# Moving the second keys' projection, four kinds of small work and seven last matmuls in an attention and FFT-filter kernel

## The chip, the cores and the metric

The kernel runs on one core of one Trainium2 chip. The time is the device time of one execution in microseconds (us): 424.93 is the median of three runs (424.67 to 424.96). Smaller is better. The core has five engines that run their own instruction lists in order and wait for each other by semaphores: PE (TensorE, matrix multiply), DVE (VectorE), ACT (ScalarE, here the exponentials), POOL (GpSimd) and SP (SyncE, here a queue that issues DMAs).

## The reference

`x` is 2048 tokens by 448 features, in bf16. Two branches are mixed by a gate:

```python
g = sigmoid((x * gate_w).sum(-1, keepdims=True))
# A: attention with 16 heads of 28
q, k, v = split(x @ wqkv)                 # (1, 16, 2048, 28) each
p = softmax(q @ k^T * 28 ** -0.5)
a = (p @ v, heads joined) @ wo
# B: a filter in the frequency domain
X = rfft2(x) * (w_r + 1j * w_i)           # (2048, 225)
b = irfft2(X).astype(bfloat16)
return g * a + (1 - g) * b
```

## The kernel before

**Attention.** The 16 heads are four groups `T` of four heads; a head is padded to 32 rows, so that a group fills 128 partitions. Queries are cut in four pieces of 512; a chunk `c` (0 to 15) is one group and one piece. For a chunk there are 16 blocks of 128 keys. A score tile is one key block, one head and 512 queries: one matmul that uses 32 rows of the PE array (`score`, L834), so that four of different heads run side by side. The scores of two or three tiles fill a PSUM buffer `ps2` or `ps3` (one of each), and one ACT instruction (L1092, in `exp`) exponentiates the whole buffer, 1024 or 1536 columns, into a tile in SBUF. There are 358 of these exponentials; "exp k" below is the k-th from 0, and "scores(k)" are the matmuls that fill its buffer. The even ones have 1536 columns and the odd ones 1024. Scores(k+2) need the buffer of exp k and so follow its end. Exponentiated tiles are multiplied with the values by four matmuls that use 32 columns each (`pv`, L1013, into the bank `psPV`). A part of the key blocks, "packs", is exponentiated on DVE instead: a score goes to a bank `bg`, L850 reads it, and a chain of DVE operations on 2048 columns follows (L870 to L904). For most packs its last addition is a DMA that POOL issues (L899).

**Other work** is cut in "units" with phases (`Unit`): a phase is a function `pe(ps)` that emits matmuls into a PSUM bank and a function `ve(ps)` that copies the result away, mostly on DVE. There are the banks `bg0` and `bg1`, and at the start also `pv`. `q`/`k` units project 512 tokens to queries or keys with four matmuls of 512 columns (`qk_unit`, L290) and one copy (L562); `first_unit` does so for group 0, with a square and a correcting matmul behind it (L614, L615, L619, L623). `T` units transpose x (L298, copied at L449). `V` units make the values of a block of 128 tokens with four matmuls of 336 columns (`v_unit`, L506) and one copy (L510). `f1`, `A`, `B`, `I` and `Z` units are the stages of the two FFTs; a `B` unit is L746 to L748 with two multiplications on DVE (L756, L758).

**The order** is decided when the program is built. `stream` goes through k: it emits exp k, some value matmuls (`do_pv`), then as many phases as a planner with assumed costs lets fit (`pick`, `step`), and then scores(k+2) (`scores`). `step` emits the matmuls and the copy at once, except for phases named in `BEHIND`: these are put in a list, `self.behind`, which is emitted behind the next scores. Matmuls on zeros fill holes that the planner sees and keep PE active: `until` and `dummy` call `one_zero` (L1328 and L1334), `zeros` adds one beside scores (L1049). None of them is read.

At the start of a group, `begin_group` spreads the projection's weights to the padded layout (`spread_w`, L285) with DVE copies; groups 1 to 3 have two such copies each. At a chunk's end `close_chunk` copies the sums out of `psPV` (L951), inverts the denominators (L961), multiplies them with the gate (L962, 128x16), and sends them by way of DRAM (SP, L966 and L975) to all rows; POOL then scales the chunk (L986, four instructions of 128x128).

Of the kernel before, what the change touches and what calls it, by code (L numbers as in the profile page):

```python
# [16 lines left out]
ALU = mybir.AluOpType  # L17
# [8 lines left out]
NT = 16  # L26
# [6 lines left out]
NC = 16  # L33
# [10 lines left out]
E_SC, E_EX, E_PV, E_PV2, E_MM = 0.32, 0.05, 0.33, 0.215, 0.22  # L44
# [8 lines left out]
BESIDE = 0.6  # L53
LATER = 70.0

BEHIND = {("T2.0", 1), ("T2.2", 1), ("q0.2", 1), ("f1.5", 1), ("I.0", 1), ("I.6", 1), ("base14", 3), ("out4", 3), ("out6", 2)}
NPT = 4
NPD = 5
CLAIM, LAST = 10, 8
# [105 lines left out]
class Kernel:  # L165
# [334 lines left out]
    def v_unit(self, t):  # L500

        nc = self.nc

        def pe(ps):
            for c in range(4):
                nc.tensor.matmul(ps[:, 0:D - DC], lhsT=self.xT[:, c, 128 * t:128 * t + 128],  # L506
                                 rhs=self.Wqkv[:, c, 2 * D + DC:3 * D], start=(c == 0), stop=(c == 3))

        def ve(ps):
            nc.vector.tensor_copy(out=self.vsb[:, t, 4:H, 0:DH],  # L510
                                  in_=ps[:, 0:D - DC].rearrange("p (h d) -> p h d", d=DH))
        return Unit(f"V{t}", [(pe, 0.68, 1344, ve, 0.42)], needs=["W3"])
# [41 lines left out]
    def qk_unit(self, T, q, b):  # L554
        nc = self.nc

        def pe(ps):
            self.project(ps, T, q, b)

        def ve(ps):  # L560
            dst = (self.kT if q else self.qT)[T][:, 512 * b:512 * b + 512]
            nc.vector.tensor_copy(out=dst, in_=ps[:])  # L562
            if b == 3:
                self.vq.insert(0, (squares, E_TT, None))

        def squares():
            sq = self.marks[f"sq{T}{q}"] = self.rot1.tile([P, S], BF16, name="sq")
            src = (self.kT if q else self.qT)[T][:]
            nc.vector.tensor_tensor(out=sq[:], in0=src, in1=src, op=ALU.mult)
            self.marks[f"sqt{T}{q}"] = self.tv + 0.1  # L570
        needs = [f"{'qk'[q]}{T}.{b - 1}"] if b else [f"Wg{T}"] if q else [f"kn{T}"]
        return Unit(f"{'qk'[q]}{T}.{b}", [(pe, 0.96, 2048, ve, 0.60)], needs=needs)

    def begin_group(self, T):

        self.new_group(T)
        for q in (1, 0):
            if T > 1:
                self.Wg[T, q] = self.Wg[T - 2, q]
            if T == 2 and q == 0:  # L580
                ones = self.Wg[T, q][:, 3, :].rearrange("p (s r) -> p s r", r=32)[:, :, KR:KR + 1]
                self.nc.gpsimd.memset(ones[96:P], 0.0)
            self.spread_w(T, q, self.nc.vector.tensor_copy)
            self.dve(0.20, True, self.tp)
        self.marks[f"Wg{T}"] = self.tv + 0.1
        if T == NG - 1:
            self.at(self.tv + 0.2, self.load_omg)
# [348 lines left out]
    def close_chunk(self, c):  # L936

        nc = self.nc
        T, qc = divmod(c, 4)
        if c == 12:  # L940
            assert all(n in self.marks for n in ("k3.3", "q3.3", "f1.15"))
            self.oT.append(self.per.tile([P, S], BF16, name="oT3", tag="xT_oT3"))
        if c >= TURN:
            f = self.rot2.tile([P, NT, 32], F32, name="ot", tag="o32")
            z = self.rot2.tile([P, NT, 32], BF16, name="oz", tag="sqh")
            self.dve(1.95)
            self.turned(c, f, z, 0, NT)
            self.marks[f"oT{c}"] = self.tv + 0.1
            return
        o32 = self.rot2.tile([P, QW], F32, name="o32")  # L950
        nc.vector.tensor_copy(out=o32[:], in_=self.psPV[:])  # L951
        r16 = self.rot2.tile([P, NT], F32, name="r16")
        nc.sync.dma_start(out=r16[:], in_=rows_of(o32[:, :], DH, 32, 4))
        st = {}

        def invert():
            if self.marks.get("gate", 1e9) > self.tv:
                self.at(self.tv + 3.0, invert)
                return
            i16 = self.rot2.tile([P, NT], F32, name="i16")  # L960
            nc.vector.reciprocal(out=i16[:], in_=r16[:])  # L961
            nc.vector.tensor_tensor(out=i16[:], in0=i16[:], in1=self.g16[:, qc, :], op=ALU.mult)  # L962
            self.dve(0.40)
            rD = self.dram.tile([4, QW], F32, name="rD")
            rv = rD[:]
            nc.sync.dma_start(out=_AP(tensor=rv.tensor, offset=rv.offset, ap=[[16, P], [1, 16]]), in_=i16[:])  # L966
            st["rv"] = rv
            self.at(self.tv + 3.0, spread)

        def spread():  # L970
            rep = st["rep"] = self.rot1.tile([P, QW], F32, name="rep", tag="rep")
            rv = st["rv"]

            for h in range(4):
                nc.sync.dma_start(out=rep[32 * h:32 * h + 32, :],  # L975
                                  in_=_AP(tensor=rv.tensor, offset=rv.offset + QW * h, ap=[[0, 32], [1, QW]]))

            self.at(self.tv + (8.0 if c < 12 else 5.0), lambda: self.jobs.append((self.tv + (8.0 if c < 12 else 2.0), scale)))

        def scale():  # L980
            o = self.oT[T][:, QW * qc:QW * qc + QW]

            nc.vector.memset(o[0:32, 0:4], 0.0)  # L983

            for e in range(0, QW, P):
                nc.gpsimd.tensor_tensor(out=o[:, e:e + P], in0=o32[:, e:e + P], in1=st["rep"][:, e:e + P], op=ALU.mult)  # L986
            self.tv += 0.07
            self.tg = max(self.tg, self.tv + 0.1, self.gen) + 1.27
            self.marks[f"oT{c}"] = self.tg + 0.1
        self.at(self.tv + 5.0, invert)  # L990
# [25 lines left out]
    def scores(self, k, end):  # L1016

        if self.act_c >= NC or not self.next_tile(k):
            return False
        t = self.tiles[k]  # L1020
        for c, i, _ in t:
            if c < 4:
                self.tp = max(self.tp, self.marks[f"q0.{c}"], self.marks[f"k0.{i // 4}"])
        start = max(self.tp, end + AP)
        if not self.away(start, [h for _, _, h in t]) and k > 1:
            self.zeros(start, [h for _, _, h in t])
        n = 2 if k % 2 else 3
        ps = self.psp.tile([P, n, QW], F32, name=f"ps{n}", tag=f"ps{n}", bufs=1)
        for _ in range(self.owed):
            self.nc.tensor.matmul(ps[:, 0, :], lhsT=self.warm[:], rhs=with_free(self.warm[:], [[0, 4], [1, P]]), start=True, stop=True)  # L1030
        self.owed = 0
        for e, (c, i, h) in enumerate(t):
            self.score(ps[:, e, :], c, i, h)
        self.ring[k] = ps
        start = max(self.tp, end + AP)
        self.tp = start + E_SC + (0.0 if isinstance(t[-1][1], int) else 0.1)
        self.add(self.tp, 128 * len(t))
        self.sc[k] = start + 0.50
        return True
# [200 lines left out]
    def step(self, u, b, limit):  # L1240
# [10 lines left out]
        ps = self.open[b][1]  # L1251
# [5 lines left out]
        if (u.name, len(u.phases)) in BEHIND:  # L1257

            self.behind.append(lambda: pe(ps))
            if ve is not None:  # L1260
                self.behind.append(lambda ve=ve: ve(ps))
                ve = self.later
            more = 1.0 if u.name == "T2.0" else 0.0
        else:
            pe(ps)
        self.tp = start + cost
# [2 lines left out]
        if ve is not None:  # L1269
# [7 lines left out]
            if u.name == "k0.1" and not u.phases and self.held:  # L1277
                self.held()
                self.held = None
                self.bank_free[0:2] = self.bank_free[1] + 0.6, self.bank_free[0]  # L1280
        if not u.phases:
            del self.open[b]
            if b == 2:
# [4 lines left out]

    def later(self, ps):
        pass  # L1290

    def take(self, u):

# [36 lines left out]
        self.dummies += 1  # L1330

    def one_zero(self):
        if self.pv_open and not self.ended:
            self.nc.tensor.matmul(self.psPV[:], lhsT=self.warm[:], rhs=with_free(self.warm[:], [[0, 4], [1, P]]), start=False, stop=False,  # L1334
                                  skip_group_check=True)
            self.add(self.tp + E_MM, 512)
# [31 lines left out]
    def stream(self):  # L1368
# [3 lines left out]
        self.fewer = self.begun = False  # L1372
        self.dummies = self.owed = 0
        self.ended, self.ot, self.held, self.next_exp = False, None, None, None
        self.behind = []
        self.pv_c, self.pv_free, self.pv_open = 0, 0.0, False
        for n in (3, 2):
            self.psp.tile([P, n, QW], F32, name=f"ps{n}", tag=f"ps{n}", bufs=1)
# [16 lines left out]
        k = -1  # L1395
        more = False
        while self.ring:
            k += 1
            if "T3.2" in self.marks and not more:
# [2 lines left out]
                e = self.per.tile([P, 14, QW], BF16, name="early2", tag="xtok_UT")  # L1402
                self.early[0].extend(e[:, 3 * j:3 * j + 3] for j in range(2))
                self.early[1].extend(e[:, 6 + 2 * j:8 + 2 * j] for j in range(4))
            self.exp(k)
            size = len(self.tiles[k])
            self.ta = end = max(self.ta, self.sc[k] + E_TAIL) + E_EXP[size]
# [22 lines left out]
            if self.act_c < NC:  # L1430
                self.until(end + AP)
            self.scores(k + 2, end)
            while self.behind:
                self.behind.pop(0)()
            self.fill_v(end - 0.2)
            self.log.append((k, end, self.tp, self.tv, len(self.vq), len(self.mand), self.dummies,
                             self.live, len([p for p in self.pieces if self.pack_t.get(p)]), self.pv_c))
# [222 lines left out]
```

## Time and profile before

| | |
|---|---|
| median of the runs | 424.93 us |
| the profiled execution's own time | 424.69 us |
| its span, first to last instruction | 422.9 us |
| busy: PE, ACT, DVE, POOL | 406.7, 411.5, 392.6, 61.3 us |
| exp 0 starts; exp 357 ends | 8.89; 416.56 us |
| ACT instructions of L1092 with tile `Pt` | 339, 385.6 us busy |
| TensorE clock granted | full in every slice |

The profile is of one execution, of which the span leaves out 1.8 us. The start of a row is when the engine began the instruction. ACT takes the next instruction in before the last one has ended, so that the durations of neighbours overlap; a matmul's duration (0.38 us at 512 columns) is modelled, and matmuls that follow each other without a wait start 0.215 us apart. "Idle before" counts only time in which no instruction of the engine was running.

### The profile page before, as it was taken

How to read it: one execution, taken by the hardware profiler on the slowest of the kernel's cores; microseconds unless marked ns; L12 is line 12 of the kernel's file. 1: busy time of each engine (PE TensorE's matmuls, PEld its weight loads, DVE VectorE, ACT ScalarE, POOL GpSimd, SP SyncE). 2: the span in 40 equal slices, each digit the busy share in tenths (PEclk: the TensorE clock that was granted, in tenths of full speed). 3: DMA queues.
4: the chain of work that ended last, by engine and by line, in shares of the span. 5: the costliest groups of instructions: out<-in, count | busy, mean ns of one | idle time of the engine just before them, and what ended most of it. 6: DMA issues, size and time to landing. Idle time of an engine off the chain costs nothing.

```text
span 422.9 us, 8345 instructions
## 1 busy us (share of the span) xinstructions
PE 406.7 (96%) x3196; PEld 144.5 (34%) x3196; DVE 392.6 (93%) x651; ACT 411.5 (97%) x369; POOL 61.3 (14%) x95
## 2 busy tenths in 40 slices
PE   8999999999999999999999999999999999999995
PEld 4343233333333333333333333333344332332232
DVE  6669989999899999999999999999999999999995
ACT  4999999999999999999999999999999999999994
POOL 6000002030100112012220100202002021310000
PEclk9999999999999999999999999999999999999999
DMA  9900301331302152375664446536553304233032
GB/s 234 180 8 2 8 27 31 90 72 32 76 15 47 24 101 59 73 169 103 153 154 96 105 103 117 112 71 109 111 146 81 77 2 91 49 76 78 22 74 67
DMA packets 32404, 34.30 MB, mean 81 GB/s; under 512 B 14988, under 2 KB 25228, under 8 KB 32332
## 3 DMA queue, kind: packets, MB, share of 16 engines
q1 hardware_dynamic: 28012, 20.21, 20.8%
q0 software_dynamic: 3600, 13.11, 17.1%
q8 instruction: 25, 0.41, 0.4%
q10 hardware_dynamic: 752, 0.44, 0.3%
q14 instruction: 15, 0.12, 0.1%
HBM read 14.85 MB, written 1.95 MB: 40 GB/s over the span
## 4 chain that ended last, share of the span: by engine, by line
PE 37%; ACT 30%; DVE 17%; issue 8%; DMA 6%; SPq 1%; DVEq 0%; ACTq 0%
ACT Pt L1092 28%; PE psPV L1013 7%; PE ps L834 6%; PE bg L834 4%; PE psPV L1334 4%; DVE Pd L850 4%; PE bg L290 3%; PE bg L1049 2%; DMA Fc<-cF 2%; DMA Wo<-in_A_wo_dram 2%; DVE pa L896 2%; ACT early L1092 2%; PE bg L678 1%; DVE U L689 1%; PE bg L506 1%
## 5 line engine op out<-in xcount | busy, mean ns | idle before, releaser
L1092 ACT ACTIVATE Pt<-ps 128x1024 bf16<-128x1024 f32 (+1 forms) x339 | 385.6, 1301 | 0.6 <-PE ps L834 0.2
L834 PE MATMUL ps<-qT,kT 32*128 32x512 bf16 (+2 forms) x926 | 143.3, 375 | 3.3 <-ACT Pt L1092 2.0
L850 DVE TENSOR_SCALAR Pd<-bg 128x512 uint16<-128x512 f32 x130 | 88.7, 683 | 5.0 <-PE ps L834 3.6
L1013 PE MATMUL psPV<-Pt,vsb 128*32 128x512 bf16 x818 | 79.9, 388 | 0.0
L834 PEld LDWEIGHTS <-kT 32*128 32x128 bf16 x1056 | 45.3, 91 | 93.7 <-issue 88.2
L899 POOL DMA_DIRECT2D Pd<-pa x25 | 23.7, 950 | 207.6 <-PE ps L834 89.0
L834 PE MATMUL bg<-qT,kT 32*128 32x512 bf16 x130 | 49.8, 383 | 1.2 <-DVE nM L651 0.4
L986 POOL TENSOR_TENSOR oT<-o,rep 128x128 bf16<-128x128 f32 x52 | 28.4, 572 | 132.3 <-DVE oT L983 73.2
L896 DVE TENSOR_TENSOR pa<-pa,n 128x2048 uint16<-128x2048 f16 (+2 forms) x33 | 40.1, 1214 | 0.6
L1013 PEld LDWEIGHTS <-vsb 128*32 128x32 bf16 x1008 | 23.1, 93 | 50.6 <-issue 50.0
L882 DVE TENSOR_TENSOR pa<-pa,n 128x2048 f16<-128x2048 f16 (+1 forms) x33 | 40.0, 1211 | 0.3
L1334 PE MATMUL psPV<-warm 128*128 128x512 bf16 x124 | 40.1, 385 | 0.0
L1049 PE MATMUL bg<-warm 32*128 32x512 bf16 x91 | 34.9, 383 | 1.4 <-DVE Pd L850 1.2
L290 PE MATMUL bg<-xT,Wg 128*128 128x512 bf16 (+1 forms) x112 | 29.6, 381 | 0.2
L873 DVE TENSOR_SCALAR Pd<-Pd 128x2048 uint16<-128x2048 uint16 (+1 forms) x33 | 23.2, 703 | 0.4
L870 DVE TENSOR_SCALAR n<-Pd 128x2048 uint16<-128x2048 uint16 (+1 forms) x33 | 22.5, 682 | 0.5
L689 DVE CAST U<-bg 128x450 bf16<-128x450 f32 x32 | 19.9, 622 | 3.1 <-PE bg L721 1.3
L885 DVE TENSOR_SCALAR pa<-pa 128x2048 f16<-128x2048 f16 (+1 forms) x33 | 22.5, 681 | 0.1
L878 DVE TENSOR_SCALAR pa<-n 128x2048 f16<-128x2048 uint16 (+1 forms) x33 | 22.3, 675 | 0.0
L1049 PEld LDWEIGHTS <-warm 32*128 32x128 bf16 x91 | 8.2, 90 | 29.0 <-issue 27.9
L787 PE MATMUL bg<-Binv,VT 128*128 128x448 bf16 x64 | 16.9, 355 | 0.2
L1092 ACT ACTIVATE early<-ps 128x1024 bf16<-128x1024 f32 (+1 forms) x13 | 15.3, 1264 | 1.0 <-PE ps L834 1.0
(189 smaller groups left out, 429.0 us busy)
## 6 DMA issues: line engine op xcount, KB each, us to landing
Pd<-pa POOLq DMA_DIRECT2D x25, 512.0 KB, 5.0
rep<-rD SPq DMA_DIRECT2D x52, 64.0 KB
CR<-cRB SPq DMA_DIRECT2D x8, 256.0 KB
UT<-U SPq DMA_DIRECT2D x16, 112.5 KB
VT<-U SPq DMA_DIRECT2D x16, 112.5 KB
CR<-cCS SPq DMA_DIRECT2D x8, 192.0 KB
xtok<-in_A_x_dram SPq DMA_DIRECT2D x3, 448.0 KB
out_dram<-fin SPq DMA_DIRECT2D x12, 112.0 KB
```

Source lines behind the costliest of these rows:

```text
L290: self.nc.tensor.matmul(ps[:], lhsT=self.Wg[T, q][0:k, c, :], rhs=self.xT[0:k, c, 512 * b:512 * b + 512], start=(c == 0), stop=(c == 3))
L689: self.nc.vector.tensor_copy(out=U[:], in_=ps[:, 0:F2])
L834: self.nc.tensor.matmul(out[:, w * j:w * j + w], lhsT=self.kT[T][32 * h:32 * h + 32, 128 * i:128 * i + 128], rhs=self.qT[T][32 * h:32 * h ...
L850: nc.vector.tensor_scalar(out=pk["t"][:, h, :], in0=ps[:], scalar1=SCALE * LOG2E * 512.0, scalar2=127.0 * 512.0, op0=ALU.mult, op1=ALU.add)
L882: v.tensor_tensor(out=st["a"], in0=st["a"], in1=st["n"], op=ALU.mult)
L896: v.tensor_tensor(out=q, in0=st["a"], in1=st["n"], op=ALU.mult)
L899: nc.gpsimd.dma_start(out=t, in_=q, accum_op=ALU.add)
L986: nc.gpsimd.tensor_tensor(out=o[:, e:e + P], in0=o32[:, e:e + P], in1=st["rep"][:, e:e + P], op=ALU.mult)
L1013: self.nc.tensor.matmul(self.psPV[32 * h:32 * h + 32, :], lhsT=self.vsb[:, i, 4 * T + h, :], rhs=pcs[h], start=first, stop=last, tile_posi ...
L1049: self.nc.tensor.matmul(ps[:], lhsT=self.warm[sl], rhs=with_free(self.warm[sl], [[0, 4], [1, P]]), start=True, stop=True, tile_position=(3 ...
L1092: self.nc.scalar.activation(out=Pt[:, 0:n, :], in_=ps[:, 0:n, :], func=ACT.Exp, scale=SCALE)
L1334: self.nc.tensor.matmul(self.psPV[:], lhsT=self.warm[:], rhs=with_free(self.warm[:], [[0, 4], [1, P]]), start=False, stop=False, skip_grou ...
```

## The change

It does four things.

1. `AFTER = {3: ("k0.1", 2)}`: scores(3) are held back until the second phase of the unit `k0.1` (the projection of tokens 512 to 1023 to keys) has been emitted; `T2.0` and, newly, `T3.0` are behind scores in that stretch. The zeros beside scores are left out up to k = 5.
2. `spread_w` of groups 1 to 3 (six copies) and the multiplication with the gate in `close_chunk` (13) go from DVE to POOL.
3. `SPARED`: one zero matmul less at each of the steps k = 0, 13, 116, 156 and 304. The planner counts it as if it were there. With the two that item 1 leaves out, the built program has seven matmuls fewer: three of L1328, two of L1334, two of L1049.
4. `ENDS`: of the units V5, V9, V15, q1.3, k2.1 and q3.0 the last of four matmuls, and of q3.2 the last two, are emitted behind the next scores, and with them the unit's copy on DVE.

The planner's decisions are otherwise the same: the same tiles stand in the same exp, and SP's list is the same. In the built order the exps concerned are those whose scores are emitted at that step: 2, 15, 118, 158, 306 (item 3) and 60, 75, 78, 88, 99, 208, 222 (item 4).

```diff
-BEHIND = {("T2.0", 1), ("T2.2", 1), ("q0.2", 1), ("f1.5", 1), ...
+BEHIND = {("T2.0", 1), ("T3.0", 1), ("T2.2", 1), ("q0.2", 1), ("f1.5", 1), ...
+SPARED = {0: 1, 13: 1, 116: 1, 156: 1, 304: 1}
+AFTER = {3: ("k0.1", 2)}
+ENDS = {"V5": 1, "V9": 1, "V15": 1, "q1.3": 1, "k2.1": 1, "q3.0": 1, "q3.2": 2}
...
-            self.spread_w(T, q, self.nc.vector.tensor_copy)
+            self.spread_w(T, q, self.nc.gpsimd.tensor_copy)
...
-            nc.vector.tensor_tensor(out=i16[:], in0=i16[:], in1=self.g16[:, qc, :], op=ALU.mult)
+            nc.gpsimd.tensor_tensor(out=i16[:], in0=i16[:], in1=self.g16[:, qc, :], op=ALU.mult)
...
-        if not self.away(start, [h for _, _, h in t]) and k > 1:
+        if not self.away(start, [h for _, _, h in t]) and k > max(AFTER) + 2:
             self.zeros(start, [h for _, _, h in t])
...
-        for e, (c, i, h) in enumerate(t):
-            self.score(ps[:, e, :], c, i, h)
+        def go():
+            for e, (c, i, h) in enumerate(t):
+                self.score(ps[:, e, :], c, i, h)
+        if k in AFTER:
+            self.after = k, go
+        else:
+            go()
...
+        elif u.name in ENDS:
+            n = 4 - ENDS[u.name]
+            pe(ps, range(n))
+            self.behind.append(lambda: pe(ps, range(n, 4)))
+            self.behind.append(lambda ve=ve: ve(ps))
+            ve = self.later
         else:
             pe(ps)
...
+        if self.after and AFTER[self.after[0]] == (u.name, len(u.phases) + 1):
+            k, go = self.after
+            self.after = None
+            go()
+            self.flush()
...
     def one_zero(self):
-        if self.pv_open and not self.ended:
+        if self.spare[self.k]:
+            self.spare[self.k] -= 1
+            self.add(self.tp + E_MM, 512)
+            self.dummies += 1
+        elif self.pv_open and not self.ended:
...
-            while self.behind:
-                self.behind.pop(0)()
+            if not self.after and k + 2 > min(AFTER) - 1:
+                self.flush()
```

More of the change, by code (lines that the diff above doesn't have):

```diff
@@ L54 @@
 LATER = 70.0
-BEHIND = {("T2.0", 1), ("T2.2", 1), ("q0.2", 1), ("f1.5", 1), ("I.0", 1), ("I.6", 1), ("base14", 3), ("out4", 3), ("out6", 2)}
+BEHIND = {("T2.0", 1), ("T3.0", 1), ("T2.2", 1), ("q0.2", 1), ("f1.5", 1), ("I.0", 1), ("I.6", 1), ("base14", 3), ("out4", 3), ("out6", 2)}
+SPARED = {0: 1, 13: 1, 116: 1, 156: 1, 304: 1}
+AFTER = {3: ("k0.1", 2)}
+ENDS = {"V5": 1, "V9": 1, "V15": 1, "q1.3": 1, "k2.1": 1, "q3.0": 1, "q3.2": 2}
 NPT = 4
@@ L502, in v_unit, with pe @@
         nc = self.nc
-        def pe(ps):
-            for c in range(4):
+        def pe(ps, part=range(4)):
+            for c in part:
                 nc.tensor.matmul(ps[:, 0:D - DC], lhsT=self.xT[:, c, 128 * t:128 * t + 128],
@@ L555, in qk_unit, with pe @@
         nc = self.nc
-        def pe(ps):
-            self.project(ps, T, q, b)
+        def pe(ps, part=range(4)):
+            self.project(ps, T, q, b, True, part)
         def ve(ps):
@@ L1290, in later, with flush @@
         pass
+    def flush(self):
+        while self.behind:
+            self.behind.pop(0)()
     def take(self, u):
@@ L1374, in stream @@
         self.ended, self.ot, self.held, self.next_exp = False, None, None, None
-        self.behind = []
+        self.behind, self.after = [], None
+        self.spare = dict.fromkeys(range(-1, 4 * NC * NT), 0) | SPARED
         self.pv_c, self.pv_free, self.pv_open = 0, 0.0, False
@@ L1404, in stream @@
                 self.early[1].extend(e[:, 6 + 2 * j:8 + 2 * j] for j in range(4))
+            self.k = k
             self.exp(k)
```

## The prediction

> **What bounds the kernel now.** I read the busy times first, then the groups of the exponentials, then the list of ACT's instructions one by one, and the timeline around each edit.
>
> ```profile
> PE 406.7 (96%) x3196; PEld 144.5 (34%) x3196; DVE 392.6 (93%) x651; ACT 411.5 (97%) x369; POOL 61.3 (14%) x95
> ...
> L1092 ACT ACTIVATE Pt<-ps 128x1536 bf16<-128x1536 f32 x170 | 257.4, 1514 | 0.5 <-PE ps L834 0.2
> ```
>
> ACT is busy 411.5 of 422.9 us, and the group shows only 0.5 us idle ahead of 170 exps. But idle time doesn't tell what a late exp costs, as neighbours overlap. In the list, a 1536-column exp that had to wait lasts 1.451 us and one that didn't up to 1.68; the ends are 1.343 apart (1536 columns) or 0.916 (1024), whichever it was. So a late start is free until the exp is at its least duration, and I count the **excess of ends**: the step from end to end beyond 1.343 or 0.916. Over all 358 exps it is 3.62 us; that is all that ACT's waits cost. At the exps that the change aims at it is, in us: exp 5 0.40, 15 0.14, 60 0.03, 75 0.04, 78 0.16, 79 0.08, 88 0.13, 99 0.10, 118 0.17, 158 0.02, 160 0.11, 208 0.23, 222 0.33, 306 0.00. PE and DVE are as full as ACT, so what is moved off one exp lands on the next.
>
> **Item 1, scores(3) behind the projection.**
>
> ```profile
> 13.20 0.69 DVE L614 CAST qraw<-bg 128x512 bf16<-128x512 f32 x1 [0.75 <-PE bg L290]
> 14.33 0.68 DVE L449 COPY xT<-pv 112x1024 bf16<-112x1024 bf16 x1
> 14.94 0.68 DVE L623 CAST kT<-bg 128x512 bf16<-128x512 f32 x1
> 15.21 1.02 ACT L1092 ACTIVATE early<-ps 128x1024 bf16<-128x1024 f32 x1 [0.29 <-PE ps L834]
> ```
>
> Exp 5 comes late because its scores, at 14.78, stand behind L619. The last L290 of k0.1 starts at 12.62, split off by scores(3). Unsplit, four matmuls run behind scores(2) (10.74): the last at 11.70, so L614 at 12.28, 0.92 earlier, and exp 5 is on time (-0.40). The transposes' copies (L449) then fill DVE from 13.41 to 14.70, so L623 starts at 14.70 instead of 14.94: only 0.24 of the 0.92 is left. Scores(6) need that kT: 15.67 becomes 15.43, and exp 6 follows by the head's 0.46 at 15.89. Exp 5's gain is kept only to that: **-0.24** (bounds 0 and -0.40).
>
> **Item 2, small pieces on GpSimd.** DVE loses 13 of L962 (0.175 each) and 6 of L285 (0.28 shown, steps of 0.18 to 0.28): about 2.8 to 4.0 us of 392.6. On POOL, idle 86%, a 112x448 copy took 0.56 in the head, and a 128x128 product (L986) 0.45 alone; a 128x16 product is not in the trace: between a small memset's 0.11 and 0.57. POOL runs in order, behind L899 (0.95) and L986; SP's send behind L962 gets its input 0.1 to 0.5 later, and L986, its reader, waits for DVE's L983 anyway (3.70 us at 89.16). The spread weights are needed 10 us or more after their copies. No exp's wait ends on these DVE pieces directly: **0** (bounds -0.3, and the rival's +0.4 below).
>
> **Item 3, five zeros.** k = 116:
>
> ```profile
> 142.81 0.81 PE L1328 MATMUL psPV<-warm 128*128 128x512 bf16 x3
> 143.55 0.39 PE L834 MATMUL ps<-qT,kT 32*128 32x512 bf16 x3
> ```
>
> Three zeros, 0.215 apart, delay scores(118); with two they start at 143.33, and exp 118's 0.17 goes: **-0.17**. k = 156: exp 158's 0.02 and part of exp 160's 0.11: **-0.07** (-0.02 to -0.13). k = 0: the zero in `pv` waits for a copy that ends at 10.37, and what remains starts no earlier: 0. k = 13: exp 15's 0.14 is an ACT instruction of its own (L491) between: 0. k = 304: scores(306) start 0.05 after exp 304's end, when their buffer comes free: 0.
>
> **Item 4, last matmuls behind scores.** Prices: full matmuls follow each other at 0.215 (512 columns) or 0.14 (336); changing between a full one and scores costs 0.31. So a split adds about 0.1 to PE, and takes 0.14 to 0.42 off the wait before the scores. The copy then comes after the scores and last matmul: 0.3 to 0.6 later. Whether that costs depends on who waits for the copy or for the bank.
>
> ```profile
> 245.91 0.38 PE L834 MATMUL bg<-qT,kT 32*128 32x512 bf16 x1
> 246.02 0.69 DVE L562 CAST qT<-bg 128x512 bf16<-128x512 f32 x1 [0.53 <-PE bg L290]
> 246.76 0.35 PE L746 MATMUL bg<-UT,CR 128*128 128x450 bf16 x1
> 247.24 0.39 PE L834 MATMUL ps<-qT,kT 32*128 32x512 bf16 x2
> ```
>
> - **q3.0.** Scores(208) go from 245.91 to 245.70: exp 208 gains its 0.23. But the last L290 goes from 245.60 to 246.02, behind them. L562 waits for it: 246.02 becomes 246.44, DVE already idle 0.53 there. Unit B's L746 uses the same bank and starts 0.05 after L562's end: 246.76 becomes 247.18. Scores(209) follow it: 247.24 to 247.66, scores(210): 248.21 to 248.63. Exp 210 now starts 0.52 after its scores' start, at 248.74 with 1.451, the least: it has no slack. It starts at 249.15: **+0.41**, exp 208's gain lost.
>
> ```profile
> 262.06 0.69 DVE L562 CAST qT<-bg 128x512 bf16<-128x512 f32 x1
> 262.82 0.36 PE L746 MATMUL bg<-UT,CR 128*128 128x450 bf16 x1
> 263.31 0.39 PE L834 MATMUL ps<-qT,kT 32*128 32x512 bf16 x2
> ...
> 264.21 0.39 PE L834 MATMUL ps<-qT,kT 32*128 32x512 bf16 x3
> ```
>
> - **q3.2**, two matmuls, again with a B unit on the same bank. L562 262.06 to 262.68, L746 263.44, scores(223) 263.93, scores(224) 264.83, exp 224 at 265.35 instead of 264.92, both by trace steps (rounded, +0.43 to 0.46): **+0.46**, exp 222's 0.33 lost.
>
> ```profile
> 77.42 0.50 DVE L510 CAST vsb<-bg 128x336 bf16<-128x336 f32 x1
> 80.30 0.68 DVE L562 CAST qT<-bg 128x512 bf16<-128x512 f32 x1
> 81.03 0.73 PE L506 MATMUL bg<-Wqkv,xT 128*128 128x336 bf16 x4
> 81.70 0.39 PE L834 MATMUL ps<-qT,kT 32*128 32x512 bf16 x3
> ```
>
> - **V5.** Exp 60 gains 0.03. L510 goes from 77.42 to 77.75; DVE has no gap up to L562 (80.30), which frees the bank for L506: 81.03 to 81.36, scores(64) 81.70 to 82.03, exp 64, with 0.03 of slack, +0.27: **+0.24** (0 if DVE's 0.33 is absorbed).
> - **V9**: its copy has DVE backlog ahead of it: 0. **V15**: 0.13 gained at exp 88, 0.07 of PE and a copy behind L882 to be made up by exp 90: 0 (-0.13 to +0.08).
> - **q1.3.** Exp 78 waits for value matmuls that free its `Pt` tile, not for scores; these (97.80) go behind the split, 98.0: **+0.20** (0 to +0.3).
> - **k2.1.** Exp 99's wait on PE is over at 122.20, yet it starts at 122.54. The same 0.34 stands ahead of exp 227 (268.21, 268.55), with 256 ACT instructions between and instruction fetches beside both. So earlier scores gain nothing, and the keys' copy, 122.01 to 122.30, reaches exp 103: **+0.15** (-0.10 to +0.25). [...]
>
> **Sum:** -0.24 -0.17 -0.07 +0.24 +0.20 +0.15 +0.41 +0.46 = **+0.98**. The profiled execution, 424.69, becomes 425.67; the median, 0.24 higher, 425.9.
>
> **Rivals.**
> 1. *All covered* (faster). The late copies and the bank cost nothing, because lighter DVE and earlier PE work run ahead to the next exps, and each exp aimed at gains its excess: 0.40 + 0.03 + 0.04 + 0.16 + 0.13 + 0.10 + 0.17 + 0.02 + 0.23 + 0.33 = 1.61; 423.3. It decides if exps 209, 210, 223 and 224 have 0.4 of slack. For: the start-by-start gaps really stand there. Against: exps 210 and 224 are at their least duration.
> 2. *Only the q3 units cost.* The 0.59 of V5, q1.3 and k2.1 is absorbed, since DVE has 3 us less to do: 425.3, no change or near its edge. For: V9 shows such slack. Against: DVE has no gap from 77.4 to 81.3.
> 3. *Port* (slower still). GpSimd's new pieces slow the DVE operations beside them:
>
> ```profile
> 89.16 2.15 POOL L986 TENSOR_TENSOR oT<-o,rep 128x128 bf16<-128x128 f32 x4 [3.70 <-DVE oT L983]
> 90.16 0.83 DVE L885 TENSOR_SCALAR pa<-pa 128x2048 f16<-128x2048 f16 x1
> 91.03 1.36 DVE L896 TENSOR_TENSOR pa<-pa,n 128x2048 uint16<-128x2048 f16 x1
> ```
>
> L885 takes 0.68 elsewhere and L896 1.22: 0.15 each, 0.19 on average over the 13 DVE operations that stretch. For 17 pieces that fall beside packs that is 3.2, 0.4 more than the 2.8 taken off: 426.3. It decides if each new piece meets a pack. [...]
> 4. *It doesn't do what it says:* exps 5 and 118 don't move. That is in the bounds of items 1 and 3.
>
> **How the numbers follow.** The sum as worked out 0.53; only q3 costs 0.20; the port 0.10; all covered 0.17. A measurement of this kernel can tell about 0.2%, 0.85 us, from no change: faster is under 424.08, slower over 425.78. The forecast lies close above the bound: of its 0.53, 0.42 slower and 0.11 same; of the second 0.16 same, 0.04 slower; the port slower; all covered 0.15 faster, 0.02 same. Together faster 0.15, same 0.29, slower 0.56. The range, 424.3 to 426.8, leaves out most of the fourth case and the worst ends of the bounds (k2.1 and q1.3 at their upper ends with the port).
>
> **What would show it.** Right: exp 5 without idle time; scores(118) at their buffer's release; L562 of q3.0 and q3.2 after 0.9 and 0.6 of idle DVE, L746 at about 0.05 after them, and exps 210 and 224 at 1.451 with an excess of ends of some 0.4; exps 64, 78 and 103 later; exp 99 still 0.34 after its wait; POOL with 19 instructions more; the total excess of ends 4.6 instead of 3.62. Wrong: L746 on time, or exps 209 to 210 and 223 to 224 with durations over the least. Then the sum falls by up to 0.87, to no change; and if exps 64, 78 and 103 stay on time too, it is faster.

## The result and the profile after

The changed kernel's median is 426.11 us over 18 runs; the kernel before had 424.88 in 18 runs beside it. The ratio of the runs is 1.0038, with a 95% interval from 1.0026 to 1.0049 (three of the 18 took 428 to 430 us; the medians alone give 1.0029). Forecast was 425.9, slower.

The profiled execution took 426.14 us, with a span of 424.1. Of its distance to the profiled execution of before, 0.16 us lies ahead of the first exp: its first exp ends at 10.51 instead of 10.35, as the transposes of x ahead of it (L347) took longer (the median of the first eight was 0.314 us instead of 0.219), and nothing of the change stands there (over the ten profiled executions that end lies between 10.35 and 11.42). Another 0.31 lies outside the span (2.09 us against 1.78), where no row shows what it is. So I compare from the end of the first exp to the end of the last, where nothing of this shows: the changed kernel needs 0.95 us more there. The sum had said 0.98.

The busy times on the page, and the two groups of exponentials with their shapes kept apart (busy us, mean ns of one, idle us before them and what ended it), after:

```profile
PE 407.0 (96%) x3189; PEld 145.3 (34%) x3189; DVE 390.5 (92%) x632; ACT 411.3 (97%) x369; POOL 71.4 (17%) x114
```

```profile
L1103 ACT ACTIVATE Pt<-ps 128x1536 bf16<-128x1536 f32 x170 | 259.9, 1529 | 0.6 <-PE psPV L1019 0.3 <-PE ps L840 0.2
L1103 ACT ACTIVATE Pt<-ps 128x1024 bf16<-128x1024 f32 x168 | 185.3, 1103 | 1.2 <-PE ps L840 1.0
```

The 1024-column group before:

```profile
L1092 ACT ACTIVATE Pt<-ps 128x1024 bf16<-128x1024 f32 x168 | 183.0, 1089 | 0.0
```

L1103 is the old L1092, L840 the old L834. POOL has its 19 instructions more, PE seven fewer. The idle time ahead of the 1536-column exps hardly changed (0.5 us before), but ahead of the 1024-column ones there is now 1.2 us idle instead of none, of which 1.0 ended with scores. The excess of ends over all exps is 4.57 us (3.62 before, 4.6 forecast). The timeline shows where the 1.0 is. Around q3.0:

```profile
245.97 0.38 PE L840 MATMUL bg<-qT,kT 32*128 32x512 bf16 x1
...
246.30 0.39 PE L296 MATMUL bg<-xT,Wg 128*128 128x512 bf16 x1
...
246.73 0.69 DVE L568 CAST qT<-bg 128x512 bf16<-128x512 f32 x1 [0.36 <-PE bg L296]
...
247.47 0.35 PE L752 MATMUL bg<-UT,CR 128*128 128x450 bf16 x1 [0.45 <-DVE qT L568]
...
247.95 0.39 PE L840 MATMUL ps<-qT,kT 32*128 32x512 bf16 x2
...
248.44 2.47 ACT L1103 ACTIVATE Pt<-ps 128x1024 bf16<-128x1024 f32 x2 [0.49 <-PE ps L840]
```

The last matmul stands behind the scores, the copy waits for it, the B unit's first matmul (L752) waits 0.45 us for the copy, scores(209) stand behind that, and ACT is idle 0.49. Up to here ACT is 0.28 later than before (end of exp 207); less that, the rows of L296, L568, L752 and scores(209) are at 246.02, 246.45, 247.19 and 247.67, where the prediction had 246.02, 246.44, 247.18 and 247.66. One sign of it is missing: DVE is idle 0.36 before L568, not 0.9, because the copy moved back in DVE's list too, and the operation of a pack that used to follow it (0.68 us) now runs first. Around q3.2 the chain is the same:

```profile
262.62 0.60 PE L296 MATMUL bg<-xT,Wg 128*128 128x512 bf16 x2
...
263.26 0.69 DVE L568 CAST qT<-bg 128x512 bf16<-128x512 f32 x1 [0.62 <-PE bg L296]
...
264.01 0.35 PE L752 MATMUL bg<-UT,CR 128*128 128x450 bf16 x1 [0.45 <-DVE qT L568]
...
264.98 2.37 ACT L1103 ACTIVATE Pt<-ps 128x1024 bf16<-128x1024 f32 x2 [0.51 <-PE ps L840]
```

### The profile page after: what moved, and what is told of

Same layout as the page of the kernel before. It is cut to its first block, busy times and chain, and to the rows that moved or that the text cites. A ratio compares the mean times of both kernels' runs of the same rounds, so it can differ in the third digit from the quotient of the medians.

```text
span 424.1 us, 8334 instructions
## 1 busy us (share of the span) xinstructions
PE 407.0 (96%) x3189; PEld 145.3 (34%) x3189; DVE 390.5 (92%) x632; ACT 411.3 (97%) x369; POOL 71.4 (17%) x114
## 4 chain that ended last, share of the span: by engine, by line
PE 46%; ACT 31%; DVE 13%; issue 7%; DMA 1%; SPq 1%; DVEq 0%; ACTq 0%
ACT Pt L1103 27%; PE psPV L1019 8%; PE ps L840 8%; PE bg L840 4%; PE psPV L1364 4%; PE bg L296 4%; PE bg L1060 3%; DVE Pd L856 3%; PE bg L512 2%; ACT early L1103 2%; PE bg L684 2%; DVE pa L902 1%; DVE U L695 1%; ACT oT L1103 1%; PE bg L718 1%
## 5 line engine op out<-in xcount | busy, mean ns | idle before, releaser
L1103 ACT ACTIVATE Pt<-ps 128x1024 bf16<-128x1024 f32 (+1 forms) x339 | 385.5, 1315 | 1.9 <-PE ps L840 1.2
L840 PE MATMUL ps<-qT,kT 32*128 32x512 bf16 (+2 forms) x926 | 142.8, 375 | 3.6 <-ACT Pt L1103 2.0
L1019 PE MATMUL psPV<-Pt,vsb 128*32 128x512 bf16 x818 | 79.9, 388 | 0.0
L840 PEld LDWEIGHTS <-kT 32*128 32x128 bf16 x1056 | 45.8, 91 | 95.2 <-issue 89.4
L840 PE MATMUL bg<-qT,kT 32*128 32x512 bf16 x130 | 49.8, 383 | 1.2 <-DVE nM L657 0.3
L1019 PEld LDWEIGHTS <-vsb 128*32 128x32 bf16 x1008 | 23.1, 93 | 50.4 <-issue 49.7
L888 DVE TENSOR_TENSOR pa<-pa,n 128x2048 f16<-128x2048 f16 (+1 forms) x33 | 39.9, 1208 | 0.3
L296 PE MATMUL bg<-xT,Wg 128*128 128x512 bf16 (+1 forms) x112 | 30.1, 381 | 0.6 <-DVE Pd L856 0.3
L879 DVE TENSOR_SCALAR Pd<-Pd 128x2048 uint16<-128x2048 uint16 (+1 forms) x33 | 23.7, 719 | 0.4
L891 DVE TENSOR_SCALAR pa<-pa 128x2048 f16<-128x2048 f16 (+1 forms) x33 | 22.4, 680 | 0.1
L884 DVE TENSOR_SCALAR pa<-n 128x2048 f16<-128x2048 uint16 (+1 forms) x33 | 22.4, 679 | 0.0
L968 POOL TENSOR_TENSOR i<-i,g 128x16 f32<-128x16 f32 x13 | 6.4, 491 | 88.5 <-DVE i L967 81.6
```

The lines of the kernel that those rows point to most:

```text
L296: self.nc.tensor.matmul(ps[:], lhsT=self.Wg[T, q][0:k, c, :], rhs=self.xT[0:k, c, 512 * b:512 * b + 512], start=(c == 0), stop=(c == 3))
L840: self.nc.tensor.matmul(out[:, w * j:w * j + w], lhsT=self.kT[T][32 * h:32 * h + 32, 128 * i:128 * i + 128], rhs=self.qT[T][32 * h:32 * h ...
L888: v.tensor_tensor(out=st["a"], in0=st["a"], in1=st["n"], op=ALU.mult)
L1019: self.nc.tensor.matmul(self.psPV[32 * h:32 * h + 32, :], lhsT=self.vsb[:, i, 4 * T + h, :], rhs=pcs[h], start=first, stop=last, tile_posi ...
L1103: self.nc.scalar.activation(out=Pt[:, 0:n, :], in_=ps[:, 0:n, :], func=ACT.Exp, scale=SCALE)
```

## Experiments

In each run I read the step of every exp's end against another kernel's, as in the prediction; each kernel has one profile, and nearly all steps that an edit leaves alone repeat within 0.02 us from kernel to kernel, while medians move by some tenths. Runs 1 to 4 were made together, and 5 to 8.

**1. Item 4 undone.**

```diff
-ENDS = {"V5": 1, "V9": 1, "V15": 1, "q1.3": 1, "k2.1": 1, "q3.0": 1, "q3.2": 2}
+ENDS = {}
```

> The changed kernel without item 4: all seven units emit their four matmuls and the copy at once. My theory (item 4 is what makes it slower; items 1 and 3 gain 0.24 + 0.24, item 2 nothing): 0.48 us below the kernel before, 424.4; exp 208 and exp 222 again late by 0.23 and 0.33 in their ends, exps 209 and 223 with no excess. Rival (the pieces on GpSimd slow DVE beside them): it stays above the kernel before, 425.2 to 425.6. Second rival (gains of items 1 and 3 are eaten before the end): 424.9.

Measured: 424.31 us, the kernel before 424.88; the ratio 0.9989 has an interval (0.9970 to 1.0007) that takes in no change, so the steps decide: from the first exp to the last it takes 0.84 us less than the kernel before. Exp 5 gains 0.40 and exp 6 gives 0.18 back; exps 118 and 160 gain 0.17 and 0.11; and two gains I had not counted, 0.07 at exp 126 and 0.17 at exp 222, come from item 2 (run 5). The excess at 209 and 223 is gone. Item 4 alone turns a gain into the loss.

**2. q3.0 and q3.2 whole, the other five split.**

```diff
-... "k2.1": 1, "q3.0": 1, "q3.2": 2}
+... "k2.1": 1}
```

> The changed kernel with q3.0 and q3.2 unsplit, the other five splits kept. My theory (each q3 split gives 0.23 or 0.33 at its exp and takes 0.6 at the next): 0.86 us less than the changed kernel, 425.2 to 425.3; excess of ends at exps 209, 223 and 227 about 0, 0 and 0.02. Rival (the five small splits cost most of it): not more than 0.3 below the changed kernel, 425.8.

Measured: 424.98 us, 1.13 below the changed kernel, and 1.02 in steps. Exp 209 is 0.60 earlier, 223 0.62, 227 0.19; exp 208 loses its 0.23, exp 222 only 0.16, since the other 0.17 had come with item 2. The rival of the small splits falls, though they too cost 0.67 (this run against run 1; 0.77 in steps).

**3. A decoy: the same PE list, but no copy waits behind scores.**

```diff
+        elif u.name in ("q3.0", "q3.2"):
+            n = 4 - ENDS[u.name]
+            pe(ps, (0, 1, 3) if n == 3 else (0, 3))
+            for _ in range(4 - n):
+                self.behind.append(self.zero_behind)
...
```

(`zero_behind`, left out here, is one matmul on zeros into `psPV`.)

> The changed kernel, with q3.0 and q3.2 doing one and two of their matmuls less (a part of the projection is left out), the copy emitted straight behind the ones that remain, and as many matmuls on zeros put behind the scores: PE's list has the same instructions in the same places, but the copy waits for no matmul behind the scores. My theory (the copy, and the bank it holds for unit B, is what costs): exps 208 and 222 keep their gain, exps 209 and 223 lose at most 0.1 instead of 0.6, B's first matmul stands within 0.1 of its place before; 1.0 us below the changed kernel, 425.1, 0.1 to 0.3 below the kernel that leaves the q3 units whole. Rival (it is PE's changes between score and full matmuls that cost): as slow as the changed kernel, 426.1, with exps 209 and 223 late by 0.5 or more.

Measured: 424.96 us, 1.15 below the changed kernel and level with run 2. Its timeline around q3.0:

```profile
245.97 0.39 PE L840 MATMUL ps<-qT,kT 32*128 32x512 bf16 x3
246.07 0.69 DVE L568 CAST qT<-bg 128x512 bf16<-128x512 f32 x1 [0.31 <-PE bg L296]
246.29 0.39 PE L1365 MATMUL psPV<-warm 128*128 128x512 bf16 x1
...
246.94 0.36 PE L752 MATMUL bg<-UT,CR 128*128 128x450 bf16 x1
```

The zero (L1365) stands where the projection's matmul stood, and PE changes between scores and full matmuls as often. But L568 starts 0.66 earlier and L752 0.53 earlier, without a wait, and exps 209 and 223 are 0.52 and 0.51 earlier than in the changed kernel. So of the 0.60 and 0.62 there, 0.5 is the copy and the bank. The rest is PE: against run 2, exp 209 keeps 0.08, 210 0.06, 223 0.11 and 227 0.19. I had expected the decoy to beat run 2 by 0.1 to 0.3, and it doesn't: PE's share alone eats the 0.22 and 0.16 that exps 208 and 222 gain.

**4. The q3 splits alone, on the kernel before.**

```diff
+ENDS = {"q3.0": 1, "q3.2": 2}
...
+        elif u.name in ENDS:
+            n = 4 - ENDS[u.name]
+            pe(ps, range(n))
+            self.behind.append(lambda: pe(ps, range(n, 4)))
+            self.behind.append(lambda ve=ve: ve(ps))
+            ve = self.later
```

> The kernel before with the splits of q3.0 and q3.2 alone. My theory: +0.86 us over the kernel before, 425.7, nearly all of the loss; exp 209 and 223 late by 0.6 in their ends. Rival (the loss comes from the sum of the small splits, or only together with the pieces on GpSimd): within 0.3 us of the kernel before.

Measured: 425.87 us, ratio 1.0026 (1.0015 to 1.0036). From first to last exp +0.87, with the steps of the changed kernel (-0.23, +0.61, +0.06; -0.33, +0.62, +0.20, -0.07). They need nothing of the rest of the change.

**5. Item 2 alone, on the kernel before.**

```diff
-            self.spread_w(T, q, self.nc.vector.tensor_copy)
+            self.spread_w(T, q, self.nc.gpsimd.tensor_copy)
-            nc.vector.tensor_tensor(out=i16[:], in0=i16[:], ...
+            nc.gpsimd.tensor_tensor(out=i16[:], in0=i16[:], ...
```

> The kernel before with item 2 alone (the 19 small pieces on GpSimd). My prediction's own value: no difference, 424.9. What the run without item 4 suggests: exps 126 and 222, which wait for work behind DVE's queue, gain 0.07 and 0.17, 0.25 us below the kernel before, 424.65. [...]

Measured: 424.80 us beside 425.00, not told apart by the medians. The steps: exps 126, 215 and 222 gain 0.07, 0.03 and 0.17, exp 178 loses 0.06, which the other kernels with these pieces do not show; from first to last exp 0.19 shorter. No step can be put down to pieces that hold up DVE. The long operations and the pieces, in this run:

```profile
L888 DVE TENSOR_TENSOR pa<-pa,n 128x2048 f16<-128x2048 f16 x32 | 38.9, 1214 | 0.3
...
L891 DVE TENSOR_SCALAR pa<-pa 128x2048 f16<-128x2048 f16 x32 | 22.0, 686 | 0.1
...
L968 POOL TENSOR_TENSOR i<-i,g 128x16 f32<-128x16 f32 x13 | 6.4, 491 | 89.5 <-DVE i L967 82.5 <-issue 6.8
...
L291 POOL COPY Wg<-Wqkv 112x448 bf16<-112x448 bf16 x6 | 3.8, 653 | 13.3 <-DMA Wqkv<-in_A_wqkv_dram 13.2
```

L888 and L891 took 1227 and 689 ns on average in the kernel before (as L882 and L885). But the means hide that the two engines do hold each other up:

```profile
75.20 0.62 DVE L649 TENSOR_REDUCE m<-bg 128x1 f32<-128x512 f32 x1
75.37 0.21 POOL L968 TENSOR_TENSOR i<-i,g 128x16 f32<-128x16 f32 x1 [2.27 <-DVE i L967]
...
107.09 0.85 POOL L291 COPY Wg<-Wqkv 112x448 bf16<-112x448 bf16 x1
107.33 1.17 DVE L879 TENSOR_SCALAR Pd<-Pd 128x2048 uint16<-128x2048 uint16 x1
...
227.09 1.16 DVE L888 TENSOR_TENSOR pa<-pa,n 128x2048 f16<-128x2048 f16 x1
227.25 1.07 POOL L968 TENSOR_TENSOR i<-i,g 128x16 f32<-128x16 f32 x1 [4.26 <-DVE i L967]
```

Beside a DVE operation that reads a PSUM bank, a product (L968) takes 0.21 or 0.22 us, little more than its 0.175 on DVE; that is so six times (twice the operation comes in only towards the end). The other seven times DVE was at work on 2048 columns in SBUF, and the product ended 0.07 after that operation, after up to 1.07 us. The other way round, L879 came while a copy (L291) was running and took 1.17 us instead of 0.68, and L884, at 108.84, took 0.88 instead of 0.68. These two cost DVE 0.7 us, against the 4.0 taken off it, and no exp is later for them.

**6. The five small splits as decoys.**

```diff
-... "k2.1": 1, "q3.0": 1, "q3.2": 2}
+... "k2.1": 1}
...
+            pe(ps, (0, 1, 3))
+            self.behind.append(lambda: self.zero_behind(336 if u.name[0] == "V" else 512))
-            pe(ps, range(n))
-            self.behind.append(lambda: pe(ps, range(n, 4)))
-            self.behind.append(lambda ve=ve: ve(ps))
-            ve = self.later
```

> The changed kernel without the q3 splits, and with V5, V9, V15, q1.3 and k2.1 doing three of their four matmuls (a quarter of each product is left out), the copy at once behind these, and one matmul on zeros of the same width behind the scores: PE's list as in the kernel with the five small splits. My theory: the copies' delay is what costs at V5 and k2.1, so that exps 64 and 103 lose at most 0.1 each instead of 0.32 and 0.21, while q1.3's 0.27 at exp 78 stays, since there the value matmuls wait for PE alone: 0.5 us below the kernel with the five small splits, 424.5. Rival (PE's extra changes between score and full matmuls cost it all): the same as with the small splits, 425.0, exps 64, 78 and 103 as late. Second rival (all of it is the copy): exp 78 on time too, 424.2.

Measured: 424.36 us, 0.62 below run 2, and 0.66 in steps. Exp 64 is 0.32 earlier, exps 102 and 103 by 0.09 and 0.21: there it was the copy. Exp 78 is late by the same amount (0.26 over run 1) and exp 90 too (0.15): there it is PE. Exp 78 in this run:

```profile
97.67 0.39 PE L840 MATMUL ps<-qT,kT 32*128 32x512 bf16 x3
97.99 0.39 PE L1357 MATMUL psPV<-warm 128*128 128x512 bf16 x1
...
98.31 0.61 PE L1019 MATMUL psPV<-Pt,vsb 128*32 128x512 bf16 x8
98.81 1.45 ACT L1103 ACTIVATE Pt<-ps 128x1536 bf16<-128x1536 f32 x1 [0.31 <-PE psPV L1019]
```

The exp is released by the value matmuls (L1019), which the full matmul behind the scores holds up, here one on zeros.

**7. One ACT instruction more near the start** (item 4 undone here too).

```diff
         nc.scalar.activation(out=scr[:], in_=scr[:], func=ACT.Exp)
+        nc.scalar.activation(out=scr[:], in_=scr[:], func=ACT.Exp)
```

> The changed kernel without item 4, and with one more tiny ACT instruction near the start, so that every later ACT instruction is one place further down the list. Theory (the 0.32 us between wait and start of exps 99, 227 and 355 belongs to a place in the list, every 256 instructions): it is gone at these three exps, or lies ahead of the wait instead, where it is hidden: exp 99's excess of 0.11 goes, 0.1 us below the kernel without item 4, 424.2. Rival (it belongs to what these exps wait for): exp 99 still starts 0.32 after its wait, no change.

Measured: 424.04 us, ratio to the kernel before 0.9974 (0.9964 to 0.9985). In run 1 exp 99's wait ends at 122.49 and it starts at 122.81; here 122.18 and 122.30, and its duration of 1.118 instead of 1.023 says that it now had time to spare. Its excess of 0.11 and exp 227's 0.02 are gone and no other step exceeds 0.02. The place in the list is the cause: with the semaphore waits that stand in ACT's list as well, exps 99 and 227 are instructions 191 and 447 of it, counted from 0, 256 apart, and one place further in this run. I was wrong to name exp 355 with them: it starts 0.70 after its wait in both runs, but only because exp 354 was still running.

**8. The shift, and other zeros taken out.**

```diff
-SPARED = {0: 1, 13: 1, 116: 1, 156: 1, 304: 1}
+SPARED = {28: 1, 116: 1, 144: 1, 156: 1, 178: 1}
```

> The changed kernel without item 4, and the zeros left out at the steps k = 28, 116, 144, 156 and 178 (those at 0, 13 and 304 are back). Theory: a zero is worth taking out only where it stands straight ahead of scores whose exp has no slack: exps 30, 146 and 180 gain 0.12, 0.03 and 0.07 of their excess, and what comes back costs nothing: 0.2 us below the kernel without item 4, 424.1. Rival (the next exps of the stretch lose what these gain): the same as without item 4, 424.3.

The kernel has the instruction of run 7 as well. Measured: 423.90 us beside 425.00, ratio 0.9974 (0.9957 to 0.9990): faster than both kernels. Against run 1, exp 30 gains 0.12, 32 another 0.08, 146 0.03 and 180 0.07, besides the shift's 0.13. The zeros put back at k = 0, 13 and 304 cost nothing that a step shows. Run 7's median is 0.14 above, too close for these two to be told apart by time; the steps are 0.28 apart.

## Why the prediction was right, and where it was not

The sign, the size and the cause held: item 4's late copies turn a gain of items 1 to 3 into a loss. By terms, in steps of the changed kernel against the kernel before:

| term | forecast | measured | exps |
|---|---|---|---|
| item 1 | -0.24 | -0.26 | 5: -0.40, 6: +0.18, 2: -0.04 |
| item 2 | 0 | -0.11 | 126: -0.07, 215: -0.03 |
| zero at k = 116 | -0.17 | -0.20 | 118, 119 |
| zero at k = 156 | -0.07 | -0.13 | 158, 160 |
| V5 | +0.24 | +0.29 | 60: -0.03, 64: +0.32 |
| V9, V15 | 0 | +0.01 | 75: -0.04, 88: -0.13, 90: +0.17 |
| q1.3 | +0.20 | +0.27 | 78 |
| k2.1 | +0.15 | +0.19 | 99: -0.11, 102, 103: +0.30 |
| q3.0 | +0.41 | +0.44 | 208: -0.23, 209: +0.60, 210: +0.06 |
| q3.2 | +0.46 | +0.41 | 222: -0.33, 223: +0.62, 227: +0.20, 232: -0.07 |

Before rounding they add up to 0.92; steps under 0.02 make up the rest of the 0.95. That the sum came so close is in part luck: it lacked some 0.4 us of gains (item 2, with the 0.17 of it that stands at exp 222, and 0.09 of the zeros) and some 0.3 of costs (q3.2, which then cost 0.59, q1.3, V5, k2.1, q3.0). Six steps or readings were mis-sized or wrong:

- **k2.1** came out near its value by two errors. I took the 0.34 us ahead of exp 99 as fixed in time, so that earlier scores would gain nothing. The row shows that it follows the wait: in the changed kernel the wait ends at 122.49 and the exp starts at 122.83, still 0.34 later, and the whole 0.11 was gained. That none of it would be was my estimate, and no run shows it. Run 7 shows that the late start belongs to the place in ACT's list: with one instruction more ahead of it, the 0.11 at exp 99 and the 0.02 at exp 227, 256 places on, are gone. The copy's price was 0.30 instead of 0.15, and run 6 shows that it was the copy.
- **Item 2** was not worth 0. On the kernel before it gains 0.19 between the first and the last exp (run 5), within my bound of 0.3. In the changed kernel 0.17 of it, at exp 222, is hidden in q3.2's gain: with item 2 in place, q3.2's split costs 0.59 (-0.16, +0.62, +0.19, -0.06 against run 2) instead of 0.41.
- **Where the q3 excess stands.** I looked for it at exps 210 and 224; it stands at 209 and 223, as ACT had used up its lead there already (both last 1.018 us in the trace before, the least for 1024 columns, so that the trace had shown it), and 0.20 of q3.2's at exp 227. Exp 227 is a later consequence: PE is 1.18 us behind its times before at scores(223) and still at scores(227), while ACT, 0.97 behind, has no lead left to hide it.
- **PE's share.** I put the split's extra 0.1 us of PE into the rows but not as a price of its own. Run 3 shows that it alone gives back what exps 208 and 222 gain, and run 6 that it is all of q1.3's and V15's loss.

- **V5.** Scores(64) 0.33 later, less 0.03 of slack, is +0.30, not +0.24: the 0.03 was taken off too often. The 0.29 measured agrees with the right sum.
- **Rival 3's rows.** I counted in them a loss on DVE alone, 0.15 at L885 and at L896; but the row of L986 merges four instructions. The one that was running when L885 came ended at 90.44, and L885 at 90.99; the next L986, begun at 90.40, took 0.91 us instead of 0.45 and ended at 91.31. So each held the other up: L885 took 0.83 instead of 0.68.

Of the rivals, "all covered" fell with exps 209 and 223, "only the q3 units cost" with exps 64, 78 and 103, and the price that rival 3 put on GpSimd's pieces with run 5, where item 2 shortens the kernel by 0.19 instead of costing 0.4. That the two engines hold each other up is there, as the rows of run 5 show: L968 took up to 1.07 us instead of 0.21, and L879 1.17 instead of 0.68. That a port is the cause, as the rival's name has it, was my guess; no run shows it. The holding up stays cheap here because only two of the 19 pieces held up DVE, while the products that waited did so on POOL, which has time (17% busy in the changed kernel). The DVE groups' means hardly tell: the worst of 32 operations, L879, went from 711 to 728 ns, and nearly all of that is the one row.

## What to carry to other kernels

Moving the end of a piece of work behind the urgent instruction moves its consumer too: ask who waits for the copy, who gets its bank next, and which urgent instruction stands behind that one on the in-order engine. A late start is worth removing only where the instruction after it has no slack, and the step from end to end shows that where idle time and start times don't. Work that nobody reads is the best thing to take away, but only where it stands straight ahead of such a start: three of the five zeros spared were worth nothing, and three others were worth 0.3 us.

## What the runs showed of the hardware

A start that comes late after its wait, at two exps 256 places apart in ACT's list, belongs to the place: 0.34 us at exps 99 and 227 in the kernel before (122.20 to 122.54, 268.21 to 268.55), and 0.32 at exp 99 in run 1. One instruction of 0.2 us put in at the head, where ACT is idle for 2.1 us anyway, moves it to where it costs nothing (run 7), and gained 0.13 us in steps. A matmul on the full array behind one on 32-row tiles cost about 0.1 us more than one that follows its like (0.32 between the starts in run 3, 245.97 to 246.29, against 0.215), and in run 3, with PE busy for 406.8 of 423.0 us, this was enough to cancel what exps 208 and 222 gain, 0.22 and 0.16. The 128x16 product on GpSimd (run 5) took 0.21 or 0.22 us beside a DVE operation that reads PSUM, and up to 1.07 beside one on 2048 columns in SBUF, which it outlasted by 0.07; the mean of 0.49 shows neither.
